# The first loads of a spectral filter with a feed-forward gate: transform constants and second-chunk rows asked for ahead of two tiles of w1, and the sixth tile of w1 later

## The chip, the core and the metric

The kernel runs on one NeuronCore of one Trainium2 chip, in one launch. The metric is the device time of one execution in microseconds (us). Five engines work beside each other, each through its own list of instructions in order: TensorE (PE in the profile; its weight loads are PEld), VectorE (DVE), ScalarE (ACT), GpSimd (POOL), and SyncE (SP), which here does nothing but ask for transfers. Sixteen DMA engines carry the transfers.

## What is computed

```python
def reference(A_x, A_w_r, A_w_i, B_x, B_w1, B_w2):
    x  = A_x                                    # (1, 2048, 1024)
    xn = layernorm(x)                           # over the last axis
    X  = rfft2(xn) * (A_w_r + 1j * A_w_i)       # over rows and d, filter (2048, 513)
    s  = irfft2(X, s=(2048, 1024))
    h  = silu(xn @ B_w1)                        # w1: (1024, 3584)
    g  = silu(h @ B_w2)                         # w2: (3584, 1024)
    return x + s * g
```

## The kernel before, in words

The 2048 rows are cut into 4 chunks of 512, and a chunk into 4 blocks of 128 rows. Every large product is made in fp16 with a value split into a high and a low half, so a product is three matmuls: high by high, high by low, low by high. Three bodies of work share the engines:

- **The feed-forward part.** w1 is taken in 28 tiles of 128 columns. `weights1` (L265) asks for a tile (`load`, L273, tile `w1r`), takes its largest absolute value on DVE (`maxi`, L277), sums that over the partitions by a small matmul and makes a power-of-two scale (`scales`, L280), then makes the high half on ACT (`split`, L296, written at L253) and the low half on DVE (`rest`, L300, written at L256). The raw tiles `w1r` and the split tiles `w1` come from one pool of seven buffers. `mm1` (L442) makes one group of 24 matmuls for chunk c and tile f (line L451): 8 slices of d for each of the three terms. The line L446 says in which order: either all of high by high, then all of (weight high, x low), then all of (weight low, x high); or, sorted, the three terms of one slice after each other. Its output goes through Silu on ACT (L460). After w1 comes the product with w2 (lines L534 to L536), made as seven products of sums and differences of quarter matrices.
- **The layer norm and the transposed chunks.** `load_x` (L652) loads a block of rows. Chunk 0 is transposed on TensorE (L742). For chunk 1 `entering` (L690) gives ACT the normalization (L733, tile `xp`) and the high half (L703, tile `xs`), DVE the low half (L711), and SP two transposing transfers per block (L706), one for the high and one for the low half, into `xnT1`. Chunks 2 and 3 go the same way through `turned` (L661, transposes at L668). The statistics of a block are DVE's (L725 to L728) and POOL's (L730 to L732).
- **The transform.** Over d: the constants `cas` are loaded by `load_fwd` (L648, issue at L649), and `fa_mat` (L782) multiplies one block of a chunk by them (L786 to L788); ACT copies the result out (L795, L796). Then come the passes over the rows, the filter and the inverse (`iu`, L1208 and L1216; DVE's butterflies from L1224 on).

Nothing is scheduled by the machine: the order of each engine's instructions is the order in which this program calls them. `slot(q)` advances a generator by one step; `wq` holds the w1 work, `bg` the layer norm and the transform. At the start SP is given the four blocks of chunk 0, then w1's first four tiles (L304). The loop at L1486 advances the two queues by turns, with idle matmuls (`spin`) between, and after it chunk 1's rows and the constants are asked for (L1489 to L1492). During the first five groups of matmuls the strings of `ENTRY` (L29) say which step comes at the 9th and the 17th matmul of a group and behind it: `f` is `fa_mat`, `e` its copy, `w` and `b` are steps of the two queues. The steps of w1's first six tiles stand in the string at L314: `m` the maximum, `p` and `s` the scales of two tiles or one, `h` the high half, `l` the low half. A step `h` of tile 1 or 2 also asks for tile 4 or 5.

Of the kernel before, what the change touches and what calls it, by code (L numbers as in the profile page):

```python
# [128 lines left out]
def spectral_ffn(ctx, tc, x, w_r, w_i, w1, w2, ca, kc, ci, tw, pm, out):  # L129
# [122 lines left out]
    def high(hi, raw, scale):  # L252
        nc.scalar.activation(hi, raw, AF.Copy, scale=scale)  # L253

    def low(lo, raw, scale, hi):
        nc.vector.scalar_tensor_tensor(lo, raw, scale, hi, op0=OP.mult, op1=OP.subtract)  # L256
# [3 lines left out]
    def column_sums(name, m, n, ones=ones):  # L260
        ps = pf.tile([128, 512], F32, name=name, tag="ff")
        nc.tensor.matmul(ps[:, 0:n], ones, m, start=True, stop=True)
        return ps[:, 0:n]

    def weights1():  # L265

        raw = {}

        def load(i):  # L273
            raw[i] = fp.tile([128, 8, 128], F32, name=f"w1r{i}", tag="w1", bufs=7)
            nc.sync.dma_start(raw[i], w1v[:, :, i * 128:(i + 1) * 128])

        def maxi(i):  # L277
            nc.vector.tensor_reduce((m1 if i < 6 else m1b)[:, i:i + 1], raw[i], axis=AX.XY, op=OP.max, apply_absolute_value=True)  # L278

        def scales(i, k):  # L280
            sl = slice(i, i + k)
            ps = column_sums(f"s1_{i}", *((m1[:, sl], k) if i < 6 else (m1b[:, sl], k, unit)))
            nc.vector.tensor_single_scalar(e1[:, sl].bitcast(I32), ps.bitcast(I32), 0x7F800000, op=OP.bitwise_and)
            nc.vector.tensor_single_scalar(e1[:, sl], e1[:, sl], 2.0**-100, op=OP.max)
            nc.vector.reciprocal(r1[:, sl], e1[:, sl])
            nc.vector.tensor_single_scalar(rs[:, sl], r1[:, sl], 2.0**14, op=OP.mult)
            nc.gpsimd.tensor_single_scalar(s1[:, sl], e1[:, sl], 2.0**-24, op=OP.mult)
            if (i + k) % 2 == 0:
                p = (i + k) // 2 - 1
                nc.vector.tensor_tensor(ep[:, p:p + 1], e1[:, 2 * p:2 * p + 1], e1[:, 2 * p + 1:2 * p + 2], op=OP.max)  # L290
                nc.vector.tensor_tensor(hs[:, p:p + 1], r1[:, 2 * p:2 * p + 1], r1[:, 2 * p + 1:2 * p + 2], op=OP.min)
                nc.gpsimd.tensor_single_scalar(hs[:, p:p + 1], hs[:, p:p + 1], 2.0**7, op=OP.mult)

        new = {}

        def split(i):  # L296
            new[i] = fp.tile([128, 2, 8, 128], F16, name=f"w1_{i}", tag="w1", bufs=7)
            high(new[i][:, 0], raw[i], rs[:, i:i + 1])

        def rest(i):  # L300
            w1t[i] = w = new.pop(i)
            low(w[:, 1], raw.pop(i), rs[:, i:i + 1], w[:, 0])

        for i in range(4):  # L304
            load(i)
        yield 0
        def whole(i):

            split(i)
            if i in (1, 2):  # L310
                load(i + 3)

        steps = {"m": maxi, "s": lambda i: scales(i, 1), "p": lambda i: scales(i, 2), "h": whole, "l": rest}
        for k in "m0 m1 p0 h0 l0 h1 l1 m2 m3 p2 h2 l2 h3 l3 m4 s4 h4 l4 m5 s5 h5 l5".split():  # L314
            steps[k[0]](int(k[1]))
            yield 0

        def ahead(i):

            if i < NFT and i not in raw and i - len(used1) <= 4:  # L320
                load(i)
                load(i + 1)

        last = None
        for i in range(6, NFT, 2):
            while i not in raw:
                ahead(i)
                yield 0
                if last is not None:
                    rest(last)  # L330
                    last = None
            maxi(i)
            if last is not None:
                rest(last)
            yield 0
            maxi(i + 1)
            yield 0
            ahead(i + 2)
            yield 0
            ahead(i + 2)  # L340
            yield 0
            scales(i, 2)
            yield 0.8
            split(i)
            ahead(i + 2)
            yield 0.2
            rest(i)
            split(i + 1)
            ahead(i + 2)
            yield 0.2  # L350
            last = i + 1
        rest(last)
# [89 lines left out]
    def mm1(c, f, between={}):  # L442
        ps = pf.tile([128, 512], F32, name=f"pa{c}_{f}", tag="ff")
        w, xt = w1t[f], xnT[c]
        terms = [(d, wh, xh) for wh, xh in ((0, 0), (0, 1), (1, 0)) for d in range(8)]
        if f > 3 or c > 1 or c and f:  # L446
            terms.sort(key=lambda k: k[0])
        for n, (d, wh, xh) in enumerate(terms):
            if n in between:
                between[n]()  # L450
            nc.tensor.matmul(ps, w[:, wh, d], xt[:, xh, d], start=(n == 0), stop=(n == 23))  # L451
        if c == 3:
            used1.add(f)
        q, g = f // 2, c // 2

        def evac():
            if (q, g) not in h32:
                h32[q, g] = H["p"].tile([128, 4, 512], F32, name=f"h32_{q}_{g}", tag="h32", bufs=2)
            hq = h32[q, g]
            nc.scalar.activation(hq[:, 2 * (c % 2) + f % 2], ps, AF.Silu, scale=s1[:, f:f + 1])  # L460
            if c % 2 and f % 2:
                return hidden(q, g)

        return evac

    def hidden(q, g):

        hq = h32.pop((q, g))
        hp = H["p"]
        sc = hs[:, q:q + 1]  # L470
        tt = nc.vector.tensor_tensor

        def split(names, src):
            n = len(names)
            o = hp.tile([128, n, 4, 2, 128], F16, name=f"ho{names[0]}_{q}_{g}", tag=f"ho{n}", bufs=1)
            ov = [o[:, :, :, k] for k in range(2)]
            sv = src.rearrange("f o (p s) -> f o p s", p=4)
            high(ov[0], sv, sc)

            def rest():  # L480
                low(ov[1], sv, sc, ov[0])
                for k, m in enumerate(names):
                    defer(1, lambda k=k, m=m: nc.sync.dma_start(
                        hd[m, g][:, :, q].rearrange("f p h s -> f p (h s)"), o[:, k].rearrange("f p h s -> f p (h s)")))

            return rest

        sums = hp.tile([128, 3, 512], F32, name=f"hr{q}_{g}", tag="hr", bufs=1)
        tt(sums[:, 0:2], hq[:, 0::2], hq[:, 1::2], op=OP.subtract)  # L489
        tt(sums[:, 2], hq[:, 0], hq[:, 3], op=OP.subtract)  # L490

        def second():
            rest_s = split(("sum_0", "sum_1", "sum_d"), sums)
            tt(hq[:, 2:0:-1], hq[:, 2:4], hq[:, 0:2], op=OP.subtract)

            def third():
                rest_h = split(("one_0", "dif_1", "dif_0", "one_3"), hq)
                rest_s()
                return rest_h

            return third

        return second
# [144 lines left out]
    def load_fwd():  # L648
        nc.sync.dma_start(A["ca"], ca)  # L649
        nc.sync.dma_start(A["tw"], tw)  # L650

    def load_x(c, p):  # L652
        tag, bufs = ("Ro", 1) if (c, p) == (0, 3) else ("x", 4)
        t_ = A["p"].tile([128, 1024], F32, name=f"x{c}_{p}", tag=tag, bufs=bufs)
        nc.sync.dma_start(t_, xs[4 * c + p])
        A["x"][c, p] = t_
# [738 lines left out]
    def slot(q):  # L1395
        while q:
            job = q[0]
            cost = job.step()
            if not job.done:
                return cost  # L1400
            if q and q[0] is job:
                q.pop(0)
        return 0
# [19 lines left out]
    with tc.manual_schedule():  # L1423
# [40 lines left out]
        def spin(n):  # L1464

            if n:
                ps = pf.tile([128, 512], F32, name="spin", tag="ff")
                for _ in range(n):
                    nc.tensor.matmul(ps[:, 0:256], idle[:, 0:128], idle, start=True, stop=True)
# [8 lines left out]
        for i in range(2, 4):  # L1478
            load_x(0, i)
        w1j = add(wq, weights1())  # L1480
        slot(wq)
        ln = [add(bg, ln_gen(0)), None, None, None]
        nc.gpsimd.memset(mhalf, -0.5)
        nc.gpsimd.memset(unit, 1.0)
        spin(WARM[0])
        for k, q in enumerate((bg, wq, bg, wq, bg, wq, wq, bg, wq, wq)):  # L1486
            slot(q)
            spin(WARM[1 + k])
        for i in range(4):  # L1489
            load_x(1, i)  # L1490
            if i == 1:
                load_fwd()  # L1492
        for c in range(1, 4):
            ln[c] = add(bg, ln_gen(c))
        for c in range(4):
# [141 lines left out]
```

## Time and profile before

| | us |
|---|---|
| median of 3 runs | 1236.73 (1236.07 to 1237.54) |
| the profiled execution | 1240.44 |
| its span, first to last instruction | 1238.7 |
| TensorE busy | 1218.5 (98%) |
| VectorE busy | 999.5 (81%) |
| ScalarE busy | 471.9 (38%) |

A row of the timeline reads: start in us, duration, engine and line, operation, output tile <- input tiles, shapes, count, and in brackets how long the engine stood idle before it and what ended that. SPq rows are transfers being asked for; the view of the transfers gives the microseconds from the asking to the landing.

### The profile page before, as it was taken

How to read it: one execution, taken by the hardware profiler on the slowest of the kernel's cores; microseconds unless marked ns; L12 is line 12 of the kernel's file. 1: busy time of each engine (PE TensorE's matmuls, PEld its weight loads, DVE VectorE, ACT ScalarE, POOL GpSimd, SP SyncE). 2: the span in 40 equal slices, each digit the busy share in tenths (PEclk: the TensorE clock that was granted, in tenths of full speed). 3: DMA queues.
4: the chain of work that ended last, by engine and by line, in shares of the span. 5: the costliest groups of instructions: out<-in, count | busy, mean ns of one | idle time of the engine just before them, and what ended most of it. 6: DMA issues, size and time to landing. Idle time of an engine off the chain costs nothing.

```text
span 1238.7 us, 19033 instructions
## 1 busy us (share of the span) xinstructions
PE 1218.5 (98%) x6992; PEld 620.3 (50%) x6992; DVE 999.5 (81%) x1974; ACT 471.9 (38%) x614; POOL 118.0 (10%) x247
## 2 busy tenths in 40 slices
PE   7999999999999999999999999999999999899998
PEld 5444445444544454445445555544455555455545
DVE  6778988798899888896969899895196778688885
ACT  5666444333555554545433222122032221243212
POOL 2320000000000000010001121113111110000000
PEclk9999999999999999999999999999999999999999
DMA  7778476645759787659898999997989999998686
GB/s 241 168 187 207 141 231 199 187 143 152 231 169 290 252 270 238 205 178 282 201 285 234 298 259 196 285 260 222 282 213 265 308 266 329 319 334 297 206 263 256
DMA packets 279550, 295.77 MB, mean 239 GB/s; under 512 B 48544, under 2 KB 207264, under 8 KB 279072
## 3 DMA queue, kind: packets, MB, share of 16 engines
q1 hardware_dynamic: 259440, 235.76, 65.0%
q10 hardware_dynamic: 15984, 51.45, 12.2%
q0 software_dynamic: 4032, 7.34, 3.5%
q8 instruction: 55, 0.90, 0.3%
q14 instruction: 39, 0.32, 0.1%
HBM read 185.95 MB, written 102.25 MB: 233 GB/s over the span
## 4 chain that ended last, share of the span: by engine, by line
PE 79%; DMA 6%; DVE 5%; ACT 3%; issue 1%; SPq 1%; ACTq 0%; DVEq 0%
PE pa L451 36%; PE pb L534 11%; PE pb L535 11%; PE pb L536 11%; DMA sd<-s 2%; PE fx L958 2%; PE id L1298 1%; DMA out_dram<-pl 1%; ACT xp L733 1%; PE fx L960 1%; PE fx L959 1%; PE iu L1216 1%; DMA jr<-in_B_w_dram 1%; DMA w1r<-in_B_w_dram 1%; PE iu L1208 1%
## 5 line engine op out<-in xcount | busy, mean ns | idle before, releaser
L451 PE MATMUL pa<-xnT,w 128*128 128x512 f16 x2688 | 584.3, 379 | 2.5 <-DMA xnT<-xs 1.7
L451 PEld LDWEIGHTS <-w 128*128 128x128 f16 x2688 | 261.4, 98 | 314.5 <-issue 1.8
L534 PE MATMUL pb<-w,ht 128*128 128x512 f16 (+2 forms) x812 | 300.9, 372 | 0.0
L535 PE MATMUL pb<-w,ht 128*128 128x512 f16 (+2 forms) x812 | 300.7, 372 | 0.0
L536 PE MATMUL pb<-w,ht 128*128 128x512 f16 (+2 forms) x812 | 300.7, 372 | 0.0
L536 PEld LDWEIGHTS <-ht 128*128 128x128 f16 x812 | 79.5, 98 | 91.3 <-issue 0.5
L534 PEld LDWEIGHTS <-ht 128*128 128x128 f16 x812 | 79.6, 98 | 86.8 <-issue 0.3
L535 PEld LDWEIGHTS <-ht 128*128 128x128 f16 x812 | 79.5, 98 | 86.8 <-issue 0.3
L460 ACT ACTIVATE h<-pa,s 128x512 f32<-128x512 f32 x112 | 75.5, 677 | 114.9 <-PE pa L451 92.1
L253 ACT ACTIVATE w<-jr,sc 128x512 f16<-128x512 f32 x98 | 68.2, 713 | 90.3 <-DMA jr<-in_B_w_dram 43.4
L253 ACT ACTIVATE hoone<-h,hs 128x2048 f16<-128x2048 f32 x28 | 55.9, 1998 | 48.5 <-issue 19.3
L256 DVE SCALAR_TENSOR_TENSOR w<-jr,sc,w 128x512 f16<-128x512 f32 x98 | 71.1, 744 | 3.8 <-ACT w L253 3.8
L253 ACT ACTIVATE hosum<-hr,hs 128x1536 f16<-128x1536 f32 x28 | 44.1, 1574 | 78.4 <-DVE hr L490 39.8
L256 DVE SCALAR_TENSOR_TENSOR hoone<-h,hs,hoone 128x2048 f16<-128x2048 f32 x28 | 65.6, 2343 | 8.2 <-ACT hoone L253 8.2
L985 ACT ACTIVATE zq<-Z,zs 128x1024 f16<-128x1024 f32 x16 | 18.4, 1149 | 93.5 <-DVE Z L1059 49.3
L256 DVE SCALAR_TENSOR_TENSOR hosum<-hr,hs,hosum 128x1536 f16<-128x1536 f32 x28 | 50.7, 1812 | 3.0 <-ACT hosum L253 3.0
L489 DVE TENSOR_TENSOR hr<-h 128x1024 f32<-128x1024 f32 x28 | 34.2, 1220 | 21.1 <-ACT h L460 21.1
L253 ACT ACTIVATE w<-w1r,rs 128x1024 f16<-128x1024 f32 x28 | 32.0, 1145 | 33.2 <-DVE w L256 22.8
L627 ACT ACTIVATE pl<-pl,c 128x512 f32<-128x512 f32 (+2 forms) x28 | 17.4, 656 | 68.1 <-DVE pl L603 47.3
L958 PE MATMUL fx<-vq,kq 128*128 128x256 f16 x192 | 43.2, 273 | 0.0
L278 DVE TENSOR_REDUCE m1b<-w1r 128x1 bf16<-128x1024 f32 x22 | 26.8, 1218 | 19.8 <-DMA w1r<-in_B_w_dram 19.8
L960 PE MATMUL fx<-vq,kq 128*128 128x128 f16 x192 | 42.1, 219 | 0.0
(225 smaller groups left out, 1529.5 us busy)
## 6 DMA issues: line engine op xcount, KB each, us to landing
w1r<-in_B_w_dram SPq DMA_DIRECT2D x28, 512.0 KB, 6.7
hd_sum<-hosum SPq DMA_DIRECT2D x56, 256.0 KB, 2.9
hd_one<-hoone SPq DMA_DIRECT2D x56, 256.0 KB, 3.7
hd_dif<-hoone SPq DMA_DIRECT2D x56, 256.0 KB, 3.4
w2m<-in_B_w_dram SPq DMA_DIRECT2D x28, 512.0 KB, 6.3
ht<-hd_dif ACTq DMA_DIRECT2D x32, 448.0 KB, 6.6
jr<-in_B_w_dram SPq DMA_DIRECT2D x56, 256.0 KB, 7.3
ht<-hd_sum ACTq DMA_DIRECT2D x32, 448.0 KB, 5.8
```

The source lines that it names most:

```text
L253: nc.scalar.activation(hi, raw, AF.Copy, scale=scale)
L256: nc.vector.scalar_tensor_tensor(lo, raw, scale, hi, op0=OP.mult, op1=OP.subtract)
L278: nc.vector.tensor_reduce((m1 if i < 6 else m1b)[:, i:i + 1], raw[i], axis=AX.XY, op=OP.max, apply_absolute_value=True)
L451: nc.tensor.matmul(ps, w[:, wh, d], xt[:, xh, d], start=(n == 0), stop=(n == 23))
L460: nc.scalar.activation(hq[:, 2 * (c % 2) + f % 2], ps, AF.Silu, scale=s1[:, f:f + 1])
L489: tt(sums[:, 0:2], hq[:, 0::2], hq[:, 1::2], op=OP.subtract)
L534: nc.tensor.matmul(ps, hh[:, 0], w[:, 0], start=first, stop=False)
L535: nc.tensor.matmul(ps, hh[:, 0], w[:, 1], start=False, stop=False)
L536: nc.tensor.matmul(ps, hh[:, 1], w[:, 0], start=False, stop=last)
L958: nc.tensor.matmul(o, k[:, c, kh, 1], v[:, c, vh], start=(n == 0), stop=False)
L960: nc.tensor.matmul(ps[:, c, 1], k[:, c, kh, 0], v[:, c, vh, 0:128], start=False, stop=(n == 2))
L985: nc.scalar.activation(zqs[q][:, 0, :, 16 * j:16 * j + 16], zs_[u], AF.Copy, scale=zs)
```

## The change

It has four parts. The fourth tile of w1 (`w1r3`) is asked for when the first maximum is taken, not ahead of it. The first two blocks of chunk 1 and the constants `cas` and `tws` are asked for before that, so ahead of `w1r3` and `w1r4`. The sixth tile (`w1r5`) is asked for behind the high half of tile 3, not of tile 2. And the groups of tile 0 with chunks 2 and 3 run their three terms unsorted.

```diff
-        for i in range(4):
+        for i in range(3):
             load(i)
         yield 0
+
+        def first(i):
+
+            maxi(i)
+            if i == 0:
+                load(3)
+
         def whole(i):
 
             split(i)
-            if i in (1, 2):
-                load(i + 3)
-
-        steps = {"m": maxi, "s": lambda i: scales(i, 1), "p": lambda i: scales(i, 2), "h": whole, "l": rest}
+            if i in (1, 3):
+                load(4 + i // 2)
+
+        steps = {"m": first, "s": lambda i: scales(i, 1), "p": lambda i: scales(i, 2), "h": whole, "l": rest}
@@
-        if f > 3 or c > 1 or c and f:
+        if f > 3 or c and f:
             terms.sort(key=lambda k: k[0])
@@
         spin(WARM[0])
+        load_x(1, 0)
         for k, q in enumerate((bg, wq, bg, wq, bg, wq, wq, bg, wq, wq)):
             slot(q)
+            if k == 0:
+                load_x(1, 1)
+                load_fwd()
             spin(WARM[1 + k])
-        for i in range(4):
+        for i in range(2, 4):
             load_x(1, i)
-            if i == 1:
-                load_fwd()
```

SP's list at its start, before. `w1r3` and `w1r4` are the fourth and fifth tile of w1, `x1_0` to `x1_3` the blocks of chunk 1, `cas` and `tws` the constants:

```order
L275 DMA w1r3_260<-in_B_w1_dram 128x8x128
L275 DMA w1r4_442<-in_B_w1_dram 128x8x128
L655 DMA x1_0_444<-in_A_x_dram 128x1024
L655 DMA x1_1_446<-in_A_x_dram 128x1024
L649 DMA cas_243<-in_ca_dram 128x2048
L650 DMA tws_244<-in_tw_dram 128x16
L655 DMA x1_2_450<-in_A_x_dram 128x1024
L655 DMA x1_3_452<-in_A_x_dram 128x1024
```

The same place in the changed kernel:

```order
L662 DMA x1_0_298<-in_A_x_dram 128x1024
L662 DMA x1_1_362<-in_A_x_dram 128x1024
L656 DMA cas_243<-in_ca_dram 128x2048
L657 DMA tws_244<-in_tw_dram 128x16
L275 DMA w1r3_376<-in_B_w1_dram 128x8x128
L275 DMA w1r4_448<-in_B_w1_dram 128x8x128
L662 DMA x1_2_450<-in_A_x_dram 128x1024
L662 DMA x1_3_452<-in_A_x_dram 128x1024
```

The four transfers from `x1_0` to `tws` now stand ahead of two tiles of w1; nothing else moved there. Next on SP come chunk 1's eight transposes, two blocks of chunk 2 and the sixth tile of w1. Before:

```order
L706 DMA_TRANSPOSE xnT1_488<-xs1_489 128x8x128 x2
L275 DMA w1r5_578<-in_B_w1_dram 128x8x128
L706 DMA_TRANSPOSE xnT1_488<-xs1_489 128x8x128 x2
L655 DMA x2_0_627<-in_A_x_dram 128x1024
L655 DMA x2_1_629<-in_A_x_dram 128x1024
L706 DMA_TRANSPOSE xnT1_488<-xs1_489 128x8x128 x4
```

And in the changed kernel:

```order
L713 DMA_TRANSPOSE xnT1_488<-xs1_489 128x8x128 x4
L662 DMA x2_0_625<-in_A_x_dram 128x1024
L662 DMA x2_1_627<-in_A_x_dram 128x1024
L275 DMA w1r5_666<-in_B_w1_dram 128x8x128
L713 DMA_TRANSPOSE xnT1_488<-xs1_489 128x8x128 x4
```

The sixth tile moved behind two transposes and two blocks of rows, and stands directly ahead of the last four transposes. It also takes another of the seven buffers of the pool, and with it the split tile `w1_3`. What ACT waits for in that stretch, before (the names in brackets are the engine or transfer counters that an instruction waits on):

```order
L253 ACTIVATE w1_2_576<-w1r2_258,rs1_225 128x1024 [waits DMAHW7_49,DVE_49]
L460 ACTIVATE h32_0_0_600<-pa0_0_454,s1_226 128x512 [waits PE_49]
L253 ACTIVATE w1_3_666<-w1r3_260,rs1_225 128x1024 [waits DMAHW0_49,DVE_49]
L733 ACTIVATE xp1_2_669<-x1_2_450,v1_2_572 128x128x8 [waits DMAHW6_49,Pool_49]
L703 ACTIVATE xs1_489<-xp1_2_669 128x1024 [waits Activation_49]
```

And in the changed kernel:

```order
L253 ACTIVATE w1_2_576<-w1r2_258,rs1_225 128x1024 [waits DMAHW7_49,DVE_49]
L467 ACTIVATE h32_0_0_598<-pa0_0_454,s1_226 128x512 [waits PE_49]
L253 ACTIVATE w1_3_664<-w1r3_376,rs1_225 128x1024 [waits DMAHW4_49]
L740 ACTIVATE xp1_2_669<-x1_2_450,v1_2_572 128x128x8 [waits DMAHW6_49,DVE_49,Pool_49]
L710 ACTIVATE xs1_489<-xp1_2_669 128x1024 [waits Activation_49]
```

The order on ACT is the same, but the high half of tile 3 no longer waits for DVE. Before, its buffer was that of the raw tile `w1r2`, which DVE's low half of tile 2 reads last; now that wait lies with SP's request for `w1r5`, and `w1_3` takes the buffer of `w1r1`. On PE, DVE, ACT and POOL no instruction changes its place, except for the order of the terms within the two groups named above.

## The prediction

> **What bounds the kernel now.** First the page's row of TensorE, then the view of who waited for whom on it (us in total, times, longest).
>
> ```profile
> PE 1218.5 (98%) x6992; PEld 620.3 (50%) x6992; DVE 999.5 (81%) x1974; ACT 471.9 (38%) x614; POOL 118.0 (10%) x247
> ```
> ```profile
> PE iu L1216 <- DVE ub L1225: 4.6, 1, 4.6
> PE fa L786 <- DMA cas<-in_ca_dram: 2.6, 1, 2.6
> ```
>
> TensorE is busy for 98% of the span, so the end moves only by what TensorE's waits lose or gain. The change does no arithmetic less; at stake are the waits of its first 110 us. The timeline of TensorE has them one by one:
>
> ```profile
> 19.27 1.90 PE L451 MATMUL pa<-xnT,w 128*128 128x512 f16 x8 [0.71 <-ACT w L253]
> 23.73 0.23 PE L786 MATMUL fa<-cas,xnT 128*128 128x128 f16 x1 [2.56 <-DMA cas<-in_ca_dram]
> ...
> 30.26 0.28 PE L262 MATMUL s<-m,ones 128*128 128x2 f32 x2
> ...
> 35.19 1.89 PE L451 MATMUL pa<-xnT,w 128*128 128x512 f16 x8
> 38.26 1.89 PE L451 MATMUL pa<-xnT,w 128*128 128x512 f16 x8
> 41.55 0.38 PE L262 MATMUL s<-m,ones 128*128 128x1 f32 x2 [1.40 <-DVE m L278]
> 41.79 7.07 PE L451 MATMUL pa<-xnT,w 128*128 128x512 f16 x32
> 49.48 0.38 PE L262 MATMUL s<-m,ones 128*128 128x1 f32 x2 [0.62 <-DVE m L278]
> 51.06 57.14 PE L451 MATMUL pa<-xnT,w 128*128 128x512 f16 x264
> 109.17 0.38 PE L451 MATMUL pa<-xnT,w 128*128 128x512 f16 x1 [0.96 <-DMA xnT<-xs]
> 110.26 20.03 PE L451 MATMUL pa<-xnT,w 128*128 128x512 f16 x92 [0.72 <-DMA xnT<-xs]
> ```
>
> **Step 1, the constants: 2.56 us.** At 23.73 TensorE waits for `cas`. The view of the transfers gives landing minus asking; ahead of each landing stands the SP row that asks (third and fifth tile of w1, first block of chunk 1, `cas`):
>
> ```profile
> 5.02 4.81 SPq L275 DMA_DIRECT2D w1r<-in_B_w_dram  x1
> ```
> ```profile
> w1r<-in_B_w_dram SPq DMA_DIRECT2D x1, 512.0 KB, 10.4
> ```
> ```profile
> 11.47 2.01 SPq L275 DMA_DIRECT2D w1r<-in_B_w_dram  x1
> ```
> ```profile
> w1r<-in_B_w_dram SPq DMA_DIRECT2D x1, 512.0 KB, 7.4
> ```
> ```profile
> 15.76 0.43 SPq L649 DMA_DIRECT2D cas<-in_ca_dram  x1
> ```
> ```profile
> cas<-in_ca_dram SPq DMA_DIRECT2D x1, 512.0 KB, 7.9
> ```
>
> The third tile lands at 5.02 + 10.4 = 15.4, the fifth at 11.47 + 7.4 = 18.9, `cas` at 15.76 + 7.9 = 23.7: they land in the order of asking. The fourth and fifth tile together take 18.9 - 15.4 = 3.5 us. Put behind `cas`, they let it land at 23.7 - 3.5 = 20.2. TensorE has done its first eight matmuls at 19.27 + 1.90 = 21.17, so the wait goes whole. If only one tile's 1.75 were won, `cas` would land at 21.9 and 0.8 us of the wait would stay. I take the whole, since the transfers follow the list. What pays: the fourth tile lands at about 20.2 + 1.75 = 22, and its maximum, the second of the two at 24.62 below, starts no earlier than 25.7 on a DVE that is busy up to there.
>
> **Step 2, the high half of tile 3: 1.40 us.** With step 1 alone the wait at 41.55 would remain. It comes from a loop over two engines:
>
> ```profile
> 24.62 2.29 DVE L278 TENSOR_REDUCE m<-w1r 128x1 f32<-128x1024 f32 x2
> ```
> ```profile
> 36.63 1.23 DVE L256 SCALAR_TENSOR_TENSOR w<-w1r,rs,w 128x1024 f16<-128x1024 f32 x1
> 39.08 1.28 DVE L256 SCALAR_TENSOR_TENSOR w<-w1r,rs,w 128x1024 f16<-128x1024 f32 x1 [1.22 <-ACT w L253]
> 40.28 1.21 DVE L278 TENSOR_REDUCE m<-w1r 128x1 f32<-128x1024 f32 x1
> ...
> 48.21 1.21 DVE L278 TENSOR_REDUCE m<-w1r 128x1 f32<-128x1024 f32 x1
> ```
> ```profile
> 32.54 1.13 ACT L253 ACTIVATE w<-w1r,rs 128x1024 f16<-128x1024 f32 x1
> ...
> 37.90 1.15 ACT L253 ACTIVATE w<-w1r,rs 128x1024 f16<-128x1024 f32 x1 [3.66 <-DVE w L256]
> ```
>
> ACT stands still for 3.66 us until DVE's low half of tile 2 frees the buffer; then DVE stands still for 1.22 us until ACT has the high half of tile 3, and the maximum behind it keeps TensorE. The rows of ACT in the section on the change show that wait gone. Step by step: the scale matmul at 30.26 moves to 27.70 (both maxima are done at 24.62 + 2.29 = 26.9), and DVE behind it by the same 2.56. ACT moves less, since its normalization needs a number of POOL:
>
> ```profile
> 24.01 0.27 POOL L732 TENSOR_SCALAR v<-mv,v 128x1 f32<-128x1 f32 x1
> ```
> ```profile
> 26.25 2.15 ACT L733 ACTIVATE xp<-x,v 128x1024 f32<-128x1024 f32 x1
> ```
>
> That starts at 24.3 for 26.25, a gain of 1.95, so the high half of tile 2 ends at 33.67 - 1.95 = 31.7, in time for TensorE at 35.19 - 2.56 = 32.63. ACT, idle before from 37.90 - 3.66 = 34.24, is free at 34.24 - 1.95 = 32.3 and makes the high half of tile 3 until 33.4. DVE: low half of tile 2 at 36.63 - 2.56 = 34.07, of tile 3 right behind it at 35.2, the maximum at 36.35 to 37.56. TensorE gets there at 38.26 + 1.89 - 2.56 = 37.59. The wait goes, by nothing to spare: a late 0.3 us there costs 0.3.
>
> **Step 3, the next maximum: 0.62 us.** ACT's next work, the normalization of chunk 1's third block, then waits for POOL's number at 36.28 - 2.56 = 33.7 and not for DVE's buffer; it and all of ACT behind it gain 38.95 - 33.74 = 5.2 us:
>
> ```profile
> 36.01 0.27 POOL L732 TENSOR_SCALAR v<-mv,v 128x1 f32<-128x1 f32 x1
> ```
> ```profile
> 38.95 2.15 ACT L733 ACTIVATE xp<-x,v 128x1024 f32<-128x1024 f32 x1
> ...
> 44.31 1.06 ACT L703 ACTIVATE xs<-xp 128x1024 f16<-128x1024 f32 x1
> ```
>
> DVE's work up to the maximum at 48.21 hangs on ACT there, so that ends at 49.42 - 5.2 = 44.2; TensorE, whose 32 matmuls end at 48.86 and gain 41.55 - 37.59 = 3.96, comes at 44.9. This needs the sixth tile. SP can ask for it at 35.3 (behind the low half of tile 2); before it took 6.7 us amid transposes, so it lands by 42.0, a microsecond ahead of 43.0.
>
> **Step 4, what is late next: chunk 1's transposes.** TensorE would begin chunk 1 at 51.06 - 4.58 = 46.48. The last two blocks' four transposes stand behind the sixth tile on SP. Their row before, and the landing of one beside a w1 tile (asked for at 34.60) and of one without (45.71):
>
> ```profile
> 42.22 6.12 SPq L706 DMA_TRANSPOSE xnT<-xs  x4
> ```
> ```profile
> xnT<-xs SPq DMA_TRANSPOSE x1, 6.8
> ```
> ```profile
> xnT<-xs SPq DMA_TRANSPOSE x1, 3.2
> ```
>
> The four wait for high halves of ACT, which gain 5.2, and low halves of DVE, which gain about 3.9 (step 2). So the first is asked for at 42.22 - 5.2 = 37.0, and the last two, at 45.7 and 47.1 before, by 41.8 and 43.2 at the latest. With 3.2 us these land by 45.0 and 46.4; TensorE needs the high ones at 46.48 and the low ones eight matmuls later, at 48.2. Bounds: 0 and about 4 us. I take 0, since the sixth tile has landed by 42.0, before the last two start.
>
> **Step 5, the unsorted groups: 0.72 us.** At 109.17 the sorted group waits for the high transposes, does one matmul and waits 0.72 for the low ones. Unsorted, eight matmuls of 0.218 (20.03 / 92) = 1.7 us lie between, so the second wait goes. The 0.96 stays: ACT has waited for TensorE before that stretch, so the chain behind moves along with it.
>
> ```profile
> 56.44 0.69 ACT L460 ACTIVATE h<-pa,s 128x512 f32<-128x512 f32 x1 [4.00 <-PE pa L451]
> ```
>
> **Sum.** 2.56 + 1.40 + 0.62 + 0.72 = 5.30. The profiled execution (1240.44, span 1238.7) would take 1235.1; the median of the runs shown is 3.7 lower, so 1236.73 - 5.30 = **1231.4**.
>
> **A rule weighed: the clock.** The one long wait late in the kernel is followed by a stretch at half the granted clock (the number ahead of the last two), the entry is not:
>
> ```profile
> 19.00:60.00 41.00, 36.15 (x240) 19.32 (x241) 29.94 (x55) 25.96 (x25) 13.56 (x31) 1.00 0.67 166
> 1066.94:1070.35 3.41, 3.41 (x25) 2.46 (x22) 2.43 (x8) 1.98 (x3) 0.00 (x0) 0.50 1.01 393
> ```
>
> So a wait of 4.6 us costs half of 3.41, 1.7 us, on top; waits of 2.56 and 1.40 cost only themselves. The Trainium skill, "TensorE: Matmul & The Clock Gate", Part 1, says that an idle window of about 3.4 us halves the clock; the trace agrees on both sides of it. By that rule no wait of the entry has a price beyond its length, and the half clock at the end goes only if that wait loses 4.64 - 3.4 = 1.2 us, which would give 1228.5 in rival E where its own estimate says 1228.7.
>
> **Rivals.**
> - *The transposes are late (A).* If one of the four again pays the 6.8 - 3.2 = 3.6 us beside the sixth tile and holds up those behind it, the high ones land at 45.0 + 3.6 = 48.6 and TensorE waits 48.6 - 46.5 = 2.1: 1231.4 + 2.1 = **1233.5**. For it: the 6.8 row. Against it: only the first of the four is asked for while the tile moves.
> - *Slower (B).* Every transpose pays that in turn; the last high one is the third, so it lands at 45.0 + 10.8 = 55.8. TensorE idles 9.3 from 46.5 and wakes at half clock, 1.7 more: 1231.4 + 11.0 = **1242.4**. From a landing at 50.1 on (3.6 of wait and 1.7 of clock use up the 5.3) it is slower than before. Against it: before, the last four, without a w1 tile beside them, took 3.2.
> - *Only the constants help (C).* The maxima stay late because DVE or ACT has another wait there: 1236.73 - 2.56 = **1234.2**.
> - *Given back later (D).* The wait of 4.6 us at the end ("iu", first view) grows by what was won: **1236.7**. For it: its last pieces in the chain of waits are transfers. Against it: the chain goes back from them to a TensorE row, so it should start earlier by the same.
>
> ```profile
> 970.63 1.35 PE iu L1208 x24
> ...
> 1024.65 13.40 DMA sd<-s
> ```
> - *The late wait gets short (E).* If these transfers come a microsecond better, the wait falls to 3.6, and perhaps the half clock goes too: 1231.4 - 1.0 - 1.7 = **1228.7**.
>
> **Chances.** Forecast 0.57; A 0.16; B 0.06; C 0.08; D 0.10; E 0.03. The forecast's own spread: 0.96 more if the wait at 109 goes as well, a microsecond less for the tight places of steps 2 and 3. The range from 1229.6 to 1234.8 holds forecast, A and C, 0.81. A measurement of this kernel tells about 0.2%, 2.5 us, from no change; faster by more than that means under 1234.26: forecast, A, E and half of C, 0.80. Within it: D and half of C, 0.14. Slower: B, 0.06.
>
> **What would show it.** In the changed profile: the first `fa` row with no wait for `cas` and starting near 21.2 (step 1); no wait of ACT for DVE at the high half of tile 3, and the two `s` rows with no wait for `m`, near 37.6 and 44.9 (steps 2, 3); the 264 matmuls from about 46.5 with no wait for `xnT` (step 4; a wait there is A or B); one wait for `xnT` near 104.6 and no second (step 5); the wait of `iu` still near 4.6 (else D or E). The forecast is wrong if the row at 51.06 moves by less than 4 us.

## The result, and the profile after

| | kernel before | changed kernel |
|---|---|---|
| median of its 6 executions, taken by turns | 1237.13 us | 1230.91 us (1228.85 to 1233.0) |
| ratio, 95% interval | | 0.9938 [0.9913, 0.9962] |
| mean over all executions of the study | 1238.19 ± 0.28 (110) | 1231.29 ± 0.46 (24) |
| lost to half clock, mean (explained below) | 2.67 ± 0.16 | 1.64 ± 0.18 |
| profiled execution, span | 1240.44, 1238.7 | 1231.15, 1229.4 |

The 110 and 24 are all executions with a listed clock, and two slow ones, 1838 us of the kernel before and 4600 us of the constants and blocks alone, are left out of every mean.

The change is faster, by more than forecast. The forecast set 5.30 us off the median of three, for 1231.4, with a range from 1229.6 on; the ratio, put on that median, gives 1229.1, a gain of 7.7 and just below that range. Its interval, 4.7 to 10.8 us, still holds 5.30; the means above, 6.9 ± 0.5 (± is a standard error throughout), don't. The direction and the mechanism of the entry, the first 110 us, were right; the step on the clock and several sizes were not.

The changed kernel's page and its view of who waited for whom on TensorE:

```profile
PE 1218.5 (99%) x6992; PEld 619.8 (50%) x6992; DVE 999.7 (81%) x1974; ACT 471.5 (38%) x614; POOL 119.7 (10%) x247
```
```profile
PE pa L458 <- DMA xnT<-xs: 0.5, 1, 0.5
...
PE iu L1223 <- DVE ub L1232: 0.2, 1, 0.2
```

TensorE does the same 1218.5 us of work. The wait for `cas` and those of `s` for `m` are in the list no more, the two waits for `xnT` (1.68 in sum) have become one of 0.5, and the wait of `iu` is 0.2 where 4.6 stood. Its timeline, for the rows that the prediction named (lines from L314 on are 7 higher than before):

```profile
19.06 1.90 PE L458 MATMUL pa<-xnT,w 128*128 128x512 f16 x8 [0.71 <-ACT w L253]
20.80 0.22 PE L793 MATMUL fa<-cas,xnT 128*128 128x128 f16 x1
...
27.32 0.28 PE L262 MATMUL s<-m,ones 128*128 128x2 f32 x2
...
37.30 0.38 PE L262 MATMUL s<-m,ones 128*128 128x1 f32 x2
...
44.45 0.31 PE L262 MATMUL s<-m,ones 128*128 128x1 f32 x2
45.95 57.28 PE L458 MATMUL pa<-xnT,w 128*128 128x512 f16 x264
103.72 22.61 PE L458 MATMUL pa<-xnT,w 128*128 128x512 f16 x104 [0.48 <-DMA xnT<-xs]
```

Up to 104 us this is the forecast's list: `fa` without a wait at 20.80 (said: 21.2), `s` at 37.30 and 44.45 (37.6 and 44.9), the 264 matmuls at 45.95 (46.5), one wait at 103.72 (104.6). Behind it stands the order on SP (asking), with the constants' landing:

```profile
11.75 0.43 SPq L656 DMA_DIRECT2D cas<-in_ca_dram  x1
...
35.19 0.58 SPq L275 DMA_DIRECT2D w1r<-in_B_w_dram  x1
36.70 7.50 SPq L713 DMA_TRANSPOSE xnT<-xs  x4
```
```profile
cas<-in_ca_dram SPq DMA_DIRECT2D x1, 512.0 KB, 7.3
```
```profile
xnT<-xs SPq DMA_TRANSPOSE x1, 3.2
```

`cas` lands at 11.75 + 7.3 = 19.1, 1.7 us ahead of its use. The four transposes are asked for from 36.70 on, and the last takes 3.2, as forecast. On ScalarE and VectorE, the loop between the two engines is gone: the high half of tile 3 (the second row at L253) follows the work ahead of it with no wait, and VectorE makes the low halves of tiles 2 and 3 back to back.

```profile
30.43 1.13 ACT L253 ACTIVATE w<-w1r,rs 128x1024 f16<-128x1024 f32 x1
31.47 0.67 ACT L467 ACTIVATE h<-pa,s 128x512 f32<-128x512 f32 x1
32.04 1.14 ACT L253 ACTIVATE w<-w1r,rs 128x1024 f16<-128x1024 f32 x1
33.37 2.22 ACT L740 ACTIVATE xp<-x,v 128x1024 f32<-128x1024 f32 x1 [0.19 <-POOL v L739]
```
```profile
33.69 2.43 DVE L256 SCALAR_TENSOR_TENSOR w<-w1r,rs,w 128x1024 f16<-128x1024 f32 x2
36.03 1.21 DVE L278 TENSOR_REDUCE m<-w1r 128x1 f32<-128x1024 f32 x1
...
43.04 1.21 DVE L278 TENSOR_REDUCE m<-w1r 128x1 f32<-128x1024 f32 x1
```

The maximum ends at 36.03 + 1.21 = 37.24 and `s` starts at 37.30, while TensorE's matmuls ahead of it (eight from 35.32, each 0.216 behind the last) leave room from 37.05 on. So the "nothing to spare" of step 2 cost a quarter of a microsecond, which shows as no wait in the row, since a matmul's drawn duration (0.38) is longer than its pitch (0.216).

### The profile page after: what moved, and what is told of

Read it like the earlier page. It is cut to its first block, busy times and chain, and to the rows that moved or that the text cites. A ratio compares the mean times of both kernels' runs of the same rounds, so it can differ in the third digit from the quotient of the medians.

```text
span 1229.4 us, 19034 instructions
## 1 busy us (share of the span) xinstructions
PE 1218.5 (99%) x6992; PEld 619.8 (50%) x6992; DVE 999.7 (81%) x1974; ACT 471.5 (38%) x614; POOL 119.7 (10%) x247
## 4 chain that ended last, share of the span: by engine, by line
PE 70%; DVE 11%; DMA 8%; issue 3%; ACT 3%; POOL 0%; SPq 0%; ACTq 0%; DVEq 0%; POOLq 0%
PE pa L458 41%; PE pb L541 8%; PE pb L543 8%; PE pb L542 8%; DVE Z L1066 2%; DMA zd<-zq 2%; PE id L1305 2%; DVE T L1031 1%; ACT xp L740 1%; DMA sd<-s 1%; DVE w L256 1%; PE iu L1215 1%; DMA ht<-hd_sum_d 1%; DMA wq<-in_A_w_i_dram 1%; DVE zq L997 1%
## 5 line engine op out<-in xcount | busy, mean ns | idle before, releaser
L253 ACT ACTIVATE w<-jr,sc 128x512 f16<-128x512 f32 x98 | 68.1, 713 | 84.4 <-DMA jr<-in_B_w_dram 35.9
L253 ACT ACTIVATE hosum<-hr,hs 128x1536 f16<-128x1536 f32 x28 | 44.1, 1574 | 78.3 <-DVE hr L497 41.4
L253 ACT ACTIVATE hoone<-h,hs 128x2048 f16<-128x2048 f32 x28 | 56.0, 1999 | 44.6 <-issue 26.5
L253 ACT ACTIVATE w<-w1r,rs 128x1024 f16<-128x1024 f32 x28 | 31.9, 1144 | 29.0 <-DVE w L256 19.1
L966 PE MATMUL fx<-vq,kq 128*128 128x128 f16 x192 | 42.0, 219 | 0.0
L967 PE MATMUL fx<-vq,kq 128*128 128x128 f16 x192 | 42.0, 219 | 0.0
```

What stands on the lines that cost most here:

```text
L966: nc.tensor.matmul(ps[:, c, 0], k[:, c, kh, 2], v[:, c, vh, 128:256], start=False, stop=False)
L967: nc.tensor.matmul(ps[:, c, 1], k[:, c, kh, 0], v[:, c, vh, 0:128], start=False, stop=(n == 2))
```

## The experiments

Open after this: which part pays what; whether the late wait of `iu`, 4.64 before and 0.23 after, belongs to the change (rival E) or to the execution; and what the change has to do with the clock. The row on half clock in the table above is the third question. The granted clock is the share of its full rate at which TensorE is allowed to run; in all profiles it is 1 or one half. Each execution lists its mean granted clock; one minus that, times the span, is the time that the half clock took from it. Up to 1.3 us of it falls behind the last matmul, where it costs nothing.

| kernel | mean, us | ratio to before [95%] | lost to half clock |
|---|---|---|---|
| before, again | 1238.3 ± 1.0 | 0.9999 [0.9975, 1.0022] | 2.7 ± 0.45 |
| changed, again | 1230.5 ± 0.7 | 0.9940 [0.9918, 0.9961] | 1.7 ± 0.4 |
| changed, third | 1232.2 ± 0.9 | 0.9952 [0.9932, 0.9972] | 1.6 ± 0.2 |
| constants and blocks alone | 1234.1 ± 0.6 | 0.9971 [0.9953, 0.9988] | 1.6 ± 0.4 |
| sixth tile alone | 1235.4 ± 0.6 | 0.9975 [0.9958, 0.9993] | 2.3 ± 0.4 |
| unsorted groups alone | 1237.0 ± 1.0 | 0.9997 [0.9977, 1.0016] | 2.6 ± 0.45 |
| changed, groups sorted | 1233.3 ± 1.0 | 0.9967 [0.9946, 0.9987] | 2.2 ± 0.5 |
| before, wait filled | 1237.5 ± 0.8 | 0.9988 [0.9969, 1.0008] | 1.75 ± 0.4 |
| wait of 3.8 | 1239.8 ± 1.0 | 1.0010 [0.9990, 1.0031] | 3.4 ± 0.5 |
| wait of 5.2 | 1241.5 ± 0.9 | 1.0025 [1.0004, 1.0046] | 4.5 ± 0.6 |
| wait of 5.2, filled | 1239.8 ± 0.6 | 1.0015 [0.9998, 1.0032] | 1.55 ± 0.4 |
| changed, group moved | 1239.1 ± 0.8 | 0.9999 [0.9981, 1.0017] | 4.2 ± 0.4 |

**Both kernels once more.** The kernel before:

> The kernel before, once more, for a second profile and for how much its own times differ. Two theories on the last third of the span, where the profile before has a wait of 4.64 us (iu, at 1066) and the changed one has 0.23 there and 0.9 at the edge sums (eps, at 838): (1) these waits differ from execution to execution of one kernel and are no part of the change: here the iu wait is anywhere between 0 and 5 us, and the times differ by up to about 5 us; (2) they belong to the order of the loads: the iu wait is 4.6 again, within 0.5, and the eps wait absent. Both: ratio 1.000 within 0.002, and the waits up to 110 us as before: 2.56, 1.40, 0.62, 1.68.

The changed kernel, and the same a third time:

> The changed kernel once more. Both theories: ratio 0.9935 to 0.9960, and no wait of TensorE over 0.6 us between 19 and 110 us. Theory 1 (late waits differ by execution): the iu wait and the eps wait may be anything from 0 to 5 us. Theory 2 (the late waits belong to the change): iu again under 0.5 us and eps again about 0.9 us.

> The changed kernel once more, beside the three others. Up to 104 us it should repeat its two profiles within 0.3 us (constants without a wait, chunk 1 near 46). Theory that the late waits belong to the execution: the wait of iu near 1059 falls anywhere between 0.2 and 4.2 with half clock behind it where it is above about 3, and the mean is 1230.7. Rival, that it belongs to the kernel: 0.23 as in the first profile.

The changed kernel's entry repeats to 0.2 us in these three profiles: chunk 1 starts at 45.95, 46.11 and 46.05. (It starts at 46.68 in the run with sorted groups below, which has the same entry and where half clock stood from 10.81 to 14.22.) The late wait does not repeat. First the changed kernel's first profile, then its second, then its third:

```profile
1058.91 0.29 PE L1223 MATMUL iu<-kk,zt 128*128 128x129 f16 x2 [0.23 <-DVE ub L1232]
```
```profile
1059.75 0.51 PE L1223 MATMUL iu<-kk,zt 128*128 128x129 f16 x3 [4.18 <-DVE ub L1232]
```
```profile
1056.27 0.92 PE L1223 MATMUL iu<-kk,zt 128*128 128x129 f16 x13 [0.93 <-DVE ub L1232]
```

The same kernel waits 0.2, 4.2 and 0.9, and the kernel before waited 4.64 and 3.99, or 0.61 with the unsorted groups. So this wait differs by the execution, and the profiled pair's 9.3 us (1240.44 to 1231.15) holds 4.4 of it by luck. So few profiles can't show that its mean is the same in both kernels. The executions can: each one's time less its loss to half clock fell, in the mean, by 5.9 ± 0.4 us, and the terms of the entry alone add up to 6.1 (below), so nothing is left for a late wait that the change makes shorter or longer. D and E both fall.

**The loads alone.** Against the changed kernel, the sixth tile and the groups are put back:

```diff
-            if i in (1, 3):
-                load(4 + i // 2)
+            if i in (1, 2):
+                load(i + 3)
@@
-        if f > 3 or c and f:
+        if f > 3 or c > 1 or c and f:
```

> Only the early loads: first two blocks of chunk 1 and the constants ahead of the fourth and fifth tile; the sixth tile and the order of the terms as before. By the steps of the prediction: the 2.56 us wait for cas goes, the waits for the maxima (1.40 and 0.62) and for the transposes at 109 (0.96 and 0.72) stay: the matmuls of chunk 1 begin at 48.5, time 2.6 us less, ratio 0.998. Rival: the three parts work only together, the waits for the maxima grow by what was won, ratio 1.000. If the late waits belong to arriving earlier (theory 2), the iu wait shrinks too and the ratio is 0.994.

```profile
39.25 0.38 PE L262 MATMUL s<-m,ones 128*128 128x1 f32 x2 [1.40 <-DVE m L278]
...
47.16 0.38 PE L262 MATMUL s<-m,ones 128*128 128x1 f32 x2 [0.61 <-DVE m L278]
48.75 57.35 PE L458 MATMUL pa<-xnT,w 128*128 128x512 f16 x264
106.65 0.38 PE L458 MATMUL pa<-xnT,w 128*128 128x512 f16 x1 [0.56 <-DMA xnT<-xs]
107.81 20.46 PE L458 MATMUL pa<-xnT,w 128*128 128x512 f16 x94 [0.78 <-DMA xnT<-xs]
```

The wait for `cas` is gone (`fa` at 21.44), and the waits of `s` stand as before, to 0.01. Step 1 is this part's, and steps 2 and 3 are not. It gains 4.1 ± 0.7 us, more than the 2.56 of its wait; the loss to half clock is down by 1.1 ± 0.4, about as in the whole change.

**The sixth tile alone.** The kernel before with

```diff
-            if i in (1, 2):
-                load(i + 3)
+            if i in (1, 3):
+                load(4 + i // 2)
```

> Only the sixth tile later. By the steps of the prediction: the wait for cas (2.56) stays, ACT no longer waits for DVE at the high half of tile 3, both waits for the maxima (1.40 and 0.62) go: the matmuls of chunk 1 begin at 49.0, time 2.0 us less, ratio 0.998. Rival: with the loads as before DVE is late anyway and the wait at 41.55 stays: ratio 1.000. Theory 2 as above.

```profile
23.22 0.23 PE L786 MATMUL fa<-cas,xnT 128*128 128x128 f16 x1 [2.00 <-DMA cas<-in_ca_dram]
...
41.38 0.38 PE L262 MATMUL s<-m,ones 128*128 128x1 f32 x2
...
48.53 0.30 PE L262 MATMUL s<-m,ones 128*128 128x1 f32 x2
50.03 57.17 PE L451 MATMUL pa<-xnT,w 128*128 128x512 f16 x264
```
```profile
34.42 1.14 ACT L253 ACTIVATE w<-w1r,rs 128x1024 f16<-128x1024 f32 x1
```

Here both waits of `s` go and the one for `cas` stays: the one line that delays the sixth tile takes 1.40 and 0.62 at once. The tiles of w1 share a pool, so the later load leaves ScalarE the buffer for which it waited 3.66 us: the high half of tile 3 (the row of ScalarE) starts without a wait. Chunk 1 starts only 1.0 earlier than in the first profile of before, since half clock stood behind the wait for `cas`, from 23.74 on, and took 1.65 back (5.81 us against 4.16 from the first `fa` matmul to the 37th behind it).

**The groups.** First unsorted in the kernel before (`if f > 3 or c and f:`), then sorted in the changed one (`if f > 3 or c > 1 or c and f:`):

> The kernel before with the unsorted groups of chunk 1 alone; constants, blocks and sixth tile stay as they were. If this part does by itself what it does in the change, the second wait for the transposed blocks near 110 us (0.72 in the kernel before) goes and the first of 0.96 stays or shrinks to about half: 0.7 to 1.4 us less, a ratio of 0.9989 to 0.9994. The wait for the constants (2.56) and those of s on ScalarE (1.40 and 0.62) stay. Rival: the order of the groups gains nothing, because the transposes come as late for the other group; then one wait of 1.5 or so stands near 109 and the ratio is 1.000.

(The edit unsorts the groups of tile 0 with chunks 2 and 3, not with chunk 1, and the waits of `s` are for DVE's maximum.)

```profile
51.57 57.27 PE L451 MATMUL pa<-xnT,w 128*128 128x512 f16 x264
109.59 18.72 PE L451 MATMUL pa<-xnT,w 128*128 128x512 f16 x86 [0.75 <-DMA xnT<-xs]
```

> The changed kernel with the sorted groups of the kernel before: constants and blocks ahead of the later tiles, sixth tile in the fourth pass. The waits for the constants and of s on ScalarE should be gone and the chunk's first matmul near 46 us as in the changed kernel (45.95); the waits for the transposed blocks near 104 should be two again, 0.5 to 1.0 and 0.7, so 0.7 to 1.4 us more than the changed kernel: a mean near 1231.7. Rival: the sorted order has no price once the blocks come early (the waits are gone in both); then the mean is the changed kernel's, 1230.7.

```profile
46.68 57.28 PE L458 MATMUL pa<-xnT,w 128*128 128x512 f16 x264
104.34 0.38 PE L458 MATMUL pa<-xnT,w 128*128 128x512 f16 x1 [0.38 <-DMA xnT<-xs]
105.49 22.84 PE L458 MATMUL pa<-xnT,w 128*128 128x512 f16 x105 [0.78 <-DMA xnT<-xs]
```

Unsorted there is one wait, sorted there are two, with the early loads and without. The second (0.72 before, 0.69 in its second profile, 0.78 here) is the order's; the first falls between 0.2 and 1.0 in the profiles that show it (one sorted profile, the filled wait of 5.2, shows only the second, of 0.82) and isn't tied to a part. The times of these two runs are too uncertain for a term of one microsecond; the rows carry it.

**What a wait does to the clock.** The loss of 1 us that went with the wait for `cas` needed a test. From the first `fa` matmul to the 37th behind it, the kernel before took 4.16 us in its first profile and 5.80 in its second. The rows below are steps of 3.41 us, three of the first profile of before, then two of the second (behind the length stands TensorE's busy time; the number ahead of the last two is the granted clock):

```profile
19.05:22.46 3.41, 1.90 (x8) 0.70 (x8) 3.30 (x6) 1.21 (x2) 0.24 (x1) 1.00 1.04 401
22.46:25.87 3.41, 2.14 (x28) 1.75 (x29) 3.31 (x6) 0.59 (x2) 2.44 (x6) 1.00 0.50 197
25.87:29.28 3.41, 3.41 (x18) 1.56 (x16) 1.05 (x1) 3.38 (x4) 0.24 (x2) 1.00 0.00 0
```
```profile
20.84:24.25 3.41, 0.81 (x7) 0.24 (x5) 2.66 (x6) 0.00 (x0) 0.97 (x1) 1.00 0.94 366
24.25:27.66 3.41, 3.41 (x27) 2.75 (x26) 3.31 (x6) 0.87 (x2) 1.95 (x7) 0.50 0.08 32
```

Same wait, 2.56 and 2.60 us; half clock behind the second only. The stretches at half clock start on a grid: in the second profile at 10.60, 24.25 and 1068.73, which is 4 and 306 steps of 3.413 apart. With the grid carried through each execution from its late stretch, the wait of the first profile falls into two steps, 1.28 and 1.27 us, and that of the second into one. Four experiments change the wait or what fills it. In the kernel before, filled:

```diff
+        if (c, p) == (0, 0):
+            for _ in range(20):
+                nc.tensor.matmul(ps[:, 0:2], idle[:, 0:128], idle, start=True, stop=True)
         for d in range(8):
             nc.tensor.matmul(ps[:, d], xt[:, 0, d, sl], A["ca"][:, 0, d], start=True, stop=False)
```

> The kernel before with 20 added matmuls of 128 columns (0.107 us each, some 2.1 in sum) into a tile that is overwritten right after, placed where TensorE waits 2.56 us for the constants. They compute nothing that is used. Theory: the wait for the constants costs more than itself, because in some executions the granted clock falls to half for 3.4 us just behind it (24.3 in one of two executions of the kernel before, +1.64 us between its matmuls there); with TensorE kept busy the half clock near 24 is never there, the first fa matmul still starts near 23.7, and the mean over the runs falls by up to 1.0 us, a mean granted clock of 0.9985 or so against 0.9978. Rival: the half clock near 24 has nothing to do with the wait, or is as rare as not to count: the mean stays at 1238.1 and the clock at 0.9978. A second rival: the added matmuls end after the constants land, and the time rises by what they overlap, up to 1 us.

(The filling matmuls, here and in the longer filling below, have 256 columns, as the row says, and start 0.109 us apart.) Their row, and the granted clock behind them:

```profile
21.80 2.35 PE L787 MATMUL fa<-ones 128*128 128x256 f16 x20
```
```profile
20.00:32.00 12.00, 11.90 (x84) 7.21 (x85) 8.46 (x18) 7.28 (x7) 3.16 (x9) 1.00 0.47 169
```

Then the constants behind three of chunk 1's blocks, behind all four, and behind all four with 42 filling matmuls:

```diff
-            if i == 1:
+            if i == 2:
                 load_fwd()
```

> The kernel before with the constants asked for behind three of the four blocks of the second chunk instead of two: the wait is between 2.56 and 5.22, about 3.9. If the loss to half clock grows with the wait (1.7 us without a wait, 2.6 with 2.56, 4.5 with 5.22), it should be about 3.6 here and the time 1.3 + 0.9 more than before: a mean near 1240.5. Rival, a threshold at a wait of about 3.4 us: every execution has the half clock here as with the long wait, and 2.56 has it never; then loss 1.7 + 1.7 to 2.5 as for the long wait.

```diff
-            if i == 1:
-                load_fwd()
+        load_fwd()
```

> The kernel before with the constants asked for behind the four blocks of x of the second chunk and not ahead of them: four more loads of about 0.64 us on the queue ahead of them, so they land some 2.6 us later and TensorE waits about 5.1 instead of 2.56. Theory that the half clock comes from the idle time, with more of it the longer the wait: half clock behind the wait in every execution, so 2.6 us and some 1 to 1.7 more: a mean near 1241.7, a ratio of 1.003. Rival: a wait costs only itself: 1240.7, ratio 1.002, and no half clock near 26 us. Second rival: the blocks that come earlier by the exchange save as much at the second chunk (waits of 0.96 and 0.72 near 109 gone): 1239.

(Two more blocks stand ahead of the constants, not four loads; the wait came out as said.)

```profile
26.14 0.29 PE L786 MATMUL fa<-cas,xnT 128*128 128x128 f16 x1 [5.22 <-DMA cas<-in_ca_dram]
```
```profile
24.61:28.02 3.41, 1.88 (x18) 1.89 (x19) 2.04 (x2) 0.00 (x0) 1.05 (x4) 0.50 0.02 7
28.02:31.43 3.41, 3.41 (x16) 1.68 (x14) 0.00 (x0) 2.52 (x3) 0.00 (x0) 0.50 0.00 0
```

> The kernel with the long wait (constants behind all four blocks of the second chunk, wait 5.22 us, mean 1241.5, mean loss to half clock 4.5 us) with 42 added matmuls of 128 columns (0.107 us each, 4.5 in sum) that keep TensorE busy through that wait; they compute nothing that is used. Theory that the idle time sets the half clock behind it: first fa matmul still near 26.1, no half clock between 24 and 32 us, loss to half clock down to about 1.7 as with the kernel whose short wait was filled (1.75), so some 2 to 2.8 us less than the long wait alone: a mean near 1239.2. Rival, the half clock has another cause (the fa matmuls themselves, the transfers): loss stays at 4.5 and the mean at 1241.5.

```profile
20.00:32.00 12.00, 12.00 (x96) 8.16 (x94) 6.96 (x10) 5.00 (x6) 2.92 (x7) 1.00 0.36 140
```

With the wait of 5.22, which fills a whole step up to 24.61 and 1.53 of the next (3.41 - 1.88), two steps are at half clock. With the filling, full clock stands throughout.

The loss to half clock grows with the wait, 1.75, 2.67, 3.4 and 4.5 us for waits of 0 (filled), 2.56, 3.83 and 5.22, and filling the longest takes it back to 1.55, though the constants come as late (first `fa` at 25.86 against 26.14). So the idle time is the cause, and the rivals that put it on the transfers or on the `fa` matmuls fall. The threshold at a wait of 3.4 falls too, with half clock behind the 2.60. The times agree as far as they can: filling gains 1.1 ± 0.9 on the short wait, and on the long one the excess over before falls from 2.9 to 1.8, each about 1 uncertain.

**A version with more.** In the changed kernel the last wait of the entry is the 0.48 at 103.72. Group (2,3) is put ahead of (3,0):

```diff
-        order += [(2, 0), (2, 1), (2, 2), (3, 0), (3, 1), (2, 3), (3, 2), (3, 3), (2, 4), (2, 5), (3, 4), (3, 5)]
+        order += [(2, 0), (2, 1), (2, 2), (2, 3), (3, 0), (3, 1), (3, 2), (3, 3), (2, 4), (2, 5), (3, 4), (3, 5)]
```

> The changed kernel with group (2,3) of the hidden layer ahead of group (3,0), the first that needs the fourth chunk's transposes: 24 matmuls of 0.216 us (5.2 us) move ahead of the place where TensorE still waited 0.30 to 0.48 us. If that wait is a transfer that lands too late, it goes whole, with the 0.16 that the record of the matmul ahead hides: 0.5 to 0.6 us less than the changed kernel, which a mean over the runs (about 1 us uncertain) will hardly show; the trace will. Rival: the group brought forward waits itself (its weight tile or ScalarE's release of a buffer), and nothing is gained.

```profile
PE fa L793 <- ACT L L803: 4.0, 1, 4.0
```

The wait goes, and TensorE is 0.8 us ahead of the changed kernel at the 601st matmul of the execution (110.09 against 110.89 in the third profile). Then at 457.43 it waits 4.0 us for ScalarE to copy out an earlier `fa`, a wait that the changed kernel doesn't have, and half clock follows at 458.02. The mean is 7.0 above that of the changed kernel beside it. Moving one group also moved the steps of the queues, so that the order of the work on TensorE, VectorE and ScalarE differs well behind the entry; which of these steps makes the wait 350 us later wasn't followed. None of the experiments beats the changed kernel.

## Why the prediction was right or wrong

**Step 1** (2.56). Right in kind: the wait went whole, and `cas` came at 19.1 where 20.2 was worked out. TensorE's first `fa` moved from 23.73 to 20.80; 0.21 of that was there at 19.27 to 19.06 already, so 2.72. The 0.16 more is hidden in every row with a wait: the matmul ahead of it is drawn 0.38 long where the next would follow after 0.22, so a wait costs its number and 0.16. The term itself varies: the four profiles with the start of the kernel before (two of it, the sixth tile alone, the unsorted groups alone) waited 2.56, 2.60, 2.00 and 1.84 us for `cas`.

**Step 2** (1.40). Measured 41.55 - 37.30 less what came before, 4.25 - 2.93 = 1.32: the 1.40 and 0.16, less the quarter of a microsecond by which the maximum was still late. **Step 3** (0.62): 0.78, again with the 0.16. That both hang on the sixth tile's load alone is shown by its run; the prediction had step 2 come from the place of the sixth tile too, and not from the earlier constants.

**Step 4** (0). Right: no wait at 45.95, and rivals A and B didn't come.

**Step 5** (0.72). Mis-sized. From the chunk's start to the 601st matmul, which lies behind both waits, the profile went from 66.12 (117.18 - 51.06) to 64.88 (110.83 - 45.95): 1.24. The second wait went with its 0.16, 0.88. The rest, 0.36, is put down to the first wait, which the prediction left at 0.96 and which was 0.48, 0.30 and 0.35 in the changed kernel's profiles and 0.96 and 0.40 before: it varies by itself, and the profile before happened to have a long one.

**The clock** is the step that failed: "waits of 2.56 and 1.40 cost only themselves". One profile of before, in which the wait happened to be cut in two by the grid, stood for all. The runs put in its place: a step of 3.41 us is followed by one at half clock when about 2 us of it were idle. In the profiles a single wait with 1.83 us in one step (the unsorted groups' `cas`, and `iu` in the last run, where 2.83 was cut into 1.83 and 1.00) had none behind it, and waits with 2.00 (the sixth tile's `cas`), 2.08, 2.15 and more all had it; behind a step that was at half clock itself, 1.53 was enough (the wait of 5.22). A wait of 2.56 that begins anywhere in the grid has 1.92 (midway between 1.83 and 2.00) or more in one step in (1.49 + 0.64) / 3.41 = 62% of its places; times half of 3.41 that is 1.07 us, an estimate, against 1.03 ± 0.24 measured (2.67 - 1.64). That it comes so close is in part luck: a wait of 1.84, which one profile had, would give nothing. The wait of 1.40 can't reach that and had no half clock in any profile. The Trainium skill, "TensorE: Matmul & The Clock Gate", Part 1, says that the window is free-running, which the grid agrees with; its idle window of about 3.4 us is not what it takes here, where 2.00 us in a step was enough.

**The sum.** By the profiles 2.72 + 1.32 + 0.78 + 0.08 (up to 45.95) + 1.24 = 6.14, and 1.03 of clock: 7.17, against 6.9 ± 0.5 between the means. The forecast's 5.30 lacks the 1.03, four times 0.16, the 0.36 of step 5 and that 0.08, and has the 0.24 of step 2 too much. The three runs of before that were shown lie below its mean over 110 (1236.73 against 1238.19), so the median of the changed kernel, 1230.91, came out nearer to 1231.4 than the terms deserve.

**Rivals.** C fell: ScalarE and VectorE had no other wait. D and E were named as effects of the change, and the late wait is none: it was 4.64 and 3.99 in the kernel before and lay between 0.2 and 4.2 in the changed one, and by the executions (5.9 ± 0.4 against 6.1) the change doesn't shorten it.

## What to carry to other kernels

Price a wait by its idle time, by what the drawn end of the instruction ahead of it hides, and by the chance that it sets half clock, which isn't zero for waits well under a step: measure that over many executions, not in one profile. Before the largest difference between two profiles is explained, take the same kernel's profile twice; here a late wait of 4.4 us was the largest and had nothing to do with the change. Where several engines share a pool of buffers, a load that is asked for later can be what lets them run.

## What the runs showed of the hardware

- Half clock comes in steps of 3.413 us on a grid that is fixed through an execution, after a step with about 2 us idle or more; a busy TensorE through the same wait keeps full clock. In the first 14 us, where transposes and idle matmuls fill the time, the border is less sharp: steps with 1.68 (sorted groups) and 1.90 us drawn idle (the second profile of before) had half clock behind them, and one with 1.69 (the first profile of before) had none.
- It also came where hardly any wait is shown. In the changed kernel's first profile the step from 837.87 has 2.97 us of drawn work, much of it small matmuls of 8 and 24 columns, and the next step is at half clock:

```profile
837.87:841.28 3.41, 2.97 (x21) 2.55 (x22) 2.13 (x9) 1.41 (x2) 2.48 (x12) 1.00 0.00 0
841.28:844.69 3.41, 3.41 (x10) 1.22 (x9) 3.41 (x5) 1.82 (x4) 2.85 (x7) 0.50 0.77 223
```

  In the filled kernel and in the one with the group moved, two steps at half clock follow the same small matmuls (from 848.91 and 847.14). Such a matmul of 8 columns is drawn 0.39 us long, as long as one of 512 columns (0.38), so the drawn time may overstate its work; whether that is the reason wasn't tried.
- The late stretch, from 822 us to the end of the `iu` wait, differs between executions of one kernel: 238.6 to 243.1 us from the 4501st to the 5941st matmul in three profiles of the changed kernel.
